# A decode step of attention plus an MLP on one core: K is transposed on VectorE in 32 by 32 blocks instead of on TensorE

## The chip, the cores and the metric

One core of a Trainium2 chip. The metric is the device time of one execution in microseconds. The kernel before takes 134.06 us (median of 8 runs, 133.88 to 134.23).

## What is computed

Two rows (batch 2, one token each, 576 wide) are normalised and go through two branches that are added. Branch A is attention with 32 query heads and 16 key/value heads over the last 2048 positions of a cache; branch B is an MLP of width 4608 with a squared ReLU.

```python
W = min(4096, max(256, Sk // 4))                       # 2048 of Sk = 8192
q = (x @ wq).reshape(B, Sq, Hq, Dh).transpose(0, 2, 1, 3)   # Hq = 32, Dh = 128
k = jnp.repeat(k_cache[:, :, Sk - W:, :], rep, axis=1)      # Hkv = 16, rep = 2
v = jnp.repeat(v_cache[:, :, Sk - W:, :], rep, axis=1)
scores = jnp.einsum("bhqd,bhkd->bhqk", q, k) * (Dh ** -0.5)
o = jnp.einsum("bhqk,bhkd->bhqd", softmax(scores), v)
A = o.transpose(0, 2, 1, 3).reshape(B, Sq, Hq * Dh) @ wo
h = relu(x @ w1 + b1) ** 2
B_ = h @ w2 + b2
out = x0 + A + B_                                      # x = layernorm(x0)
```

All inputs are bf16. 53.6 MB are read: K and V 16.8 MB each, wq and wo 4.7 MB each, w1 and w2 5.3 MB each.

## The kernel before, in words

**Units.** K and V are worked in 8 units u of 4 key/value heads and one batch row. A unit's K, and its V, is one tile of 128 partitions by 8192 elements (2 MB): each partition holds 64 consecutive positions of one head, 128 elements each. Six such tiles share one ring of buffers (`kvpool`, L85); a load into a buffer waits until the tile in it has been read for the last time.

**Loads.** All large loads are issued by SP (SyncE), in program order: k0, wq, k1, v0, k2, v1, k3, v2, k4, v3, k5, v4, k6, v5, w1, k7, v6, v7, wo, w2 in five pieces. wq, w1 and wo share one buffer (`wbig`), so w1 waits until q is computed, and wo until `mlp_h` has read w1.

**One unit.** `transposes` (L258): TensorE turns 128x128 blocks of K seen as 4-byte words (two bf16 each), four to a PSUM tile, 32 in a unit; ScalarE (L270) and VectorE (L272) in turn copy the tiles to SBUF, 8 copies a unit. `scores` (L274) multiplies by q in two halves of the unit, t = 0 and 1, on 32-column strips of TensorE that run side by side: the stationary tile is q for 8 (head, query) columns, placed by zeros (`qz`), and a product with `far_h` first puts a large negative number where head and row do not belong together. `softmax` (L288): VectorE takes the row maximum (m1, L291), spreads it (m2, L293), GpSimd takes the maximum over partitions (L295), VectorE forms the bias (gown, L298), ScalarE the exponential (L302), VectorE transposes the result in 32 by 32 blocks (pT, L305). `pv` (L314) multiplies by V in 16 products; `pv_end` (L326) sums four parts on VectorE (L333, L335); `fin` adds over partitions by a product (op, L341) and divides (L344, L347, L351), which leaves a column block of `ws`.

**Order.** TensorE keeps the program's order (L94, L97). In `step(u)` (L387) the transposes of unit u are interleaved with p·v of unit u-2 and its `fin`; scores(u, 0) comes after the sixth group of transposes, scores(u, 1) and softmax(u) at the end. VectorE's and ScalarE's order is set by a scheduler. After step 6 comes `mlp_h` (L356): 72 products with w1, ReLU on ScalarE (L373), the square on VectorE (hrow, L375), transposes back and copies to `hT_sb` (L384). Then the loads of wo and w2 are issued, and step 7, p·v of units 6 and 7, and the output products follow: 128 with wo (which need all of `ws`), 144 with w2, a cast (L456) and the store.

`q_block` (L226) computes q in 36 products when wq is there, copies it (L238), transposes it (4 products) and writes it into `qz` (L254).

Of the kernel before, what the change touches and what calls it, by code (L numbers as in the profile page):

```python
# [16 lines left out]
def kernel(  # L17
# [32 lines left out]
    JG = 8  # L50
    NG = NJ // JG
# [5 lines left out]
    TG = NG // NT  # L57
    QZ = 2 * NC
    assert SR == 32 and NG % NT == 0

# [34 lines left out]

    def transpose(*a, **k):
        tc.keep_in_program_order(nc.tensor.transpose(*a, **k))  # L97
# [18 lines left out]
    def issue_flat(w, name):  # L116
        n = w.shape[0] * w.shape[1] // P
        tl = wbig.tile([P, NH * L1], BF16, tag="wbig", name=name)
        nc.sync.dma_start(out=tl[:, 0:n], in_=w.rearrange("r n -> (r n)").rearrange("(p l) -> p l", p=P))
        return tl  # L120

    const.tile([P, 144], F32, name="pad_0")
# [15 lines left out]
    tmp_f = work.tile([P, 2, Dh], F32, tag="tmp", name="tmp_f")  # L138
# [50 lines left out]
    nc.vector.tensor_scalar(out=off[:], in0=own[:], scalar1=BIG, scalar2=-BIG, op0=ALU.mult, op1=ALU.add)  # L189
    of_h = const.tile([P, NC * WC], F32, name="of_h")  # L190
# [29 lines left out]

    qz = const.tile([P, NQ, B, 2, 3 * QZ], BF16, name="qz")
    nc.gpsimd.memset(qz[:], 0.0)
# [3 lines left out]
    def q_block():  # L226
        for t in range(NH):
            for g in range(NG4):
                o = t * LQ + g * QW
                matmul(q_ps[32 * g:32 * g + 2 * B, :], lhsT=xnT[:, t].rearrange("p x b -> p (x b)"),  # L230
                       rhs=wq_sb[:, o:o + QW], start=(t == 0), stop=(t == NH - 1), skip_group_check=True,
                       tile_position=(0, 32 * g))
        row_t = const.tile([RB, 4 * HW], BF16, tag="row", name="qrow")
        qrow = row_t[:, 0:2 * QW]
        nh = QH // 2
        for k in range(2):
            cp = nc.scalar.copy if k else nc.vector.tensor_copy
            cp(out=qrow[:, k * QW:(k + 1) * QW].rearrange("p (i a d) -> p i a d", a=2, d=Dh),  # L238
               in_=q_ps[0:RB, k * QW // 2:(k + 1) * QW // 2].rearrange("p (i d) -> p i d", d=Dh).unsqueeze(2)
               .to_broadcast([RB, nh, 2, Dh]))  # L240
        qrow_f = qrow.bitcast(F32)
        qT_ps = psum.tile([P, QH * P], F32, tag="sc", bufs=2, name="qT_ps")
        for i in range(QH):
            transpose(out=qT_ps[:, i * P:i * P + RB], in_=qrow_f[:, i * Dh:(i + 1) * Dh],
                      identity=ident_f[0:RB, 0:RB])
        qT_v = qT_ps[:].bitcast(BF16).rearrange("p (i g e x b c) -> p b x g c e i", g=NG4 // 2, e=2, x=32 // B, b=B, c=2)
        hd = Dh // 2
        for j2 in range(2):
            cp = nc.scalar.copy if j2 else nc.vector.tensor_copy
            pp = slice(hd * j2, hd * (j2 + 1))  # L250
            o = QZ + NC * j2
            for b in range(B):
                for half in range(2):
                    cp(out=qz[pp, half * NQ // 2:(half + 1) * NQ // 2, b, :, o:o + NC].rearrange(  # L254
                        "p g c (e i) -> p g c e i", e=2), in_=qT_v[pp, b, half])

    kT_tiles, sc_tiles, pT_tiles, o1_tiles, o_tiles = {}, {}, {}, {}, {}
    def transposes(u, g):  # L258
        k_f = k_tiles[u][:].bitcast(F32)
        kT_ps = psum.tile([P, JG * P], BF16, tag="kT", bufs=3, name=f"kT_ps_{u}_{g}")  # L260
        kT_f = kT_ps[:].bitcast(F32)
        for i in range(JG // 2):
            j = g * JG // 2 + i
            transpose(out=kT_f[:, i * P:(i + 1) * P], in_=k_f[:, j * P:(j + 1) * P], identity=ident_f[:])
        t, o = divmod(g, TG)
        if o == 0:
            kT_tiles[(u, t)] = ktpool.tile([P, TG * JG * P], BF16, tag="kT_sb", name=f"kT_{u}_{t}")
        kT = kT_tiles[(u, t)][:, o * JG * P:(o + 1) * JG * P]
        if g % 2 == 0:
            nc.scalar.copy(out=kT, in_=kT_ps[:])  # L270
        else:
            nc.vector.tensor_copy(out=kT, in_=kT_ps[:])  # L272

    def scores(u, t):  # L274
        tq, b = divmod(u, B)
        if t == 0:
            sc_tiles[u] = psum.tile([P, NJJ * 32], F32, tag="sc", bufs=2, name=f"sc_ps_{u}")
            matmul(sc_tiles[u][:], lhsT=far_h[:], rhs=is_h, start=True, stop=False, skip_group_check=True)
        sc_ps = sc_tiles[u]
        kT = kT_tiles.pop((u, t))[:].rearrange("p (j k c) -> p j k c", k=P, c=2)  # L280
        z = QZ * (1 - t)
        for c in range(2):
            for g in range(4):
                matmul(sc_ps[32 * g:32 * (g + 1), :], lhsT=qz[:, tq, b, c, z:z + SR],
                       rhs=kT[:, :, 32 * g:32 * (g + 1), c], start=False, stop=(t == NT - 1 and c == 1),
                       skip_group_check=True, tile_position=(0, 32 * g))

    def softmax(u):  # L288
        sc_ps = sc_tiles.pop(u)
        m1 = work.tile([P, 1], F32, tag="m1", name=f"m1_{u}")  # L290
        nc.vector.tensor_reduce(out=m1[:], in_=sc_ps[:], axis=AX.X, op=ALU.max)  # L291
        m2 = work.tile([P, NC], F32, tag="m2", name=f"m2_{u}")
        nc.vector.tensor_scalar(out=m2[:], in0=off[:], scalar1=m1[:, 0:1], scalar2=None, op0=ALU.add)  # L293
        gmax = work.tile([P, NC], F32, tag="gmax", name=f"gmax_{u}")
        nc.gpsimd.partition_all_reduce(gmax[:], m2[:], channels=P, reduce_op=ReduceOp.max)  # L295
        gown = work.tile([P, NC], F32, tag="gown", name=f"gown_{u}")
        bias = work.tile([P, 1], F32, tag="bias", name=f"bias_{u}")
        nc.vector.scalar_tensor_tensor(out=gown[:], in0=gmax[:], scalar=-scale, in1=own[:], op0=ALU.mult,  # L298
                                       op1=ALU.mult, accum_out=bias[:])
        p_sb = work.tile([P, NJJ * 32], BF16, tag="p_sb", bufs=1, name=f"p_{u}")  # L300
        o1 = keep.tile([P, Dh + 1], F32, tag="o1", name=f"o1_{u}")
        nc.scalar.activation(out=p_sb[:], in_=sc_ps[:], func=ACT.Exp, bias=bias[:, 0:1], scale=scale,  # L302
                             accum_out=o1[:, Dh:Dh + 1])
        pT = keep.tile([P, NJJ, SR], BF16, tag="pT", name=f"pT_{u}")
        nc.vector.transpose(out=pT[:].rearrange("p j r -> p (j r)"), in_=p_sb[:])  # L305
        pT_tiles[u] = pT
        o1_tiles[u] = o1
# [6 lines left out]
    def pv(u, part, parts):  # L314
        n = NJJ // parts
        if part == 0:
            o_tiles[u] = psum.tile([P, NS * Dh], F32, tag="o", name=f"o_ps_{u}")
        v = v_tiles[u][:].rearrange("p (t j s d) -> p j t s d", t=NT, s=2, d=Dh)
        for j in range(part * n, (part + 1) * n):
# [3 lines left out]
        if part == parts - 1:  # L323
            pT_tiles.pop(u)

    def pv_end(u):  # L326
# [3 lines left out]
        for k in range(NS):  # L330
            kw = dict(out=o1[:, 0:Dh], in0=o_ps[:, k * Dh:(k + 1) * Dh])
            if k == 0:
                nc.vector.tensor_scalar(scalar1=in_s[:, 0:1], scalar2=None, op0=ALU.mult, **kw)  # L333
            else:
                nc.vector.scalar_tensor_tensor(scalar=in_s[:, k:k + 1], in1=o1[:, 0:Dh], op0=ALU.mult, op1=ALU.add,  # L335
                                               **kw)

        def fin():
# [5 lines left out]
            nc.vector.reciprocal(out=linv[pp, :], in_=op[pp, Dh:Dh + 1])  # L344
            om_t = work.tile([P, Dh], F32, tag="om", name=f"om_{u}")
            om = om_t[pp, :].rearrange("p (q r) -> p q r", r=WR)
            nc.vector.scalar_tensor_tensor(out=om, in0=op[pp, 0:Dh].rearrange("p (q r) -> p q r", r=WR),  # L347
                                           scalar=linv[pp, 0:1], op0=ALU.mult, op1=ALU.mult,
                                           in1=own_c[pp, :].unsqueeze(2).to_broadcast([32, WC, WR]))
            with nc.allow_low_precision(reason="sums of one term and zeros"):  # L350
                nc.vector.tensor_reduce(out=ws[pp, :, BS * b], in_=om.rearrange("p q r -> p r q"), axis=AX.X,  # L351
                                        op=ALU.add)
# [3 lines left out]
    def mlp_h(w1_sb):  # L356
        h_ps = [psum.tile([P, HB], F32, tag="kT", bufs=3, name=f"h_ps_{k}") for k in range(2)]
# [29 lines left out]
    def step(u):  # L387
        fin = None
        w = u - 2
        with_pv = w >= 0  # L390
        for g in range(NG):
            transposes(u, g)
            if with_pv and g == 1:
                pv(w, 0, 2)
            if with_pv and g == 2:
                pv(w, 1, 2)
                fin = pv_end(w)
            if g == TG + 1:
                scores(u, 0)
            if g == TG + 2 and fin:  # L400
                fin()
        scores(u, 1)
        softmax(u)

    def pv_all(u):
        pv(u, 0, 1)
        pv_end(u)()

    for g in range(NG):
        transposes(0, g)  # L410
    q_block()
    for t in range(NT):
        scores(0, t)
    softmax(0)
    load_v(2)
    b1_rows = B_b1.rearrange("(x n) -> x n", n=HW)
# [4 lines left out]
    load_k(4)  # L421
# [16 lines left out]
    nc.sync.dma_start(out=w2a_sb[:], in_=w2_rows[0])  # L438
# [49 lines left out]
```

## Time and profile before

| | |
|---|---|
| median of 8 runs | 134.06 us (133.88 to 134.23) |
| the profiled execution's own time | 134.23 us |
| its span in the profile | 132.3 us |
| TensorE busy (949 products), weight loads | 84.1 us (64%), 52.0 us |
| VectorE busy (176 instructions) | 63.2 us (48%) |
| ScalarE busy (67 instructions) | 46.7 us (35%) |
| GpSimd busy | 4.9 us (4%) |
| HBM read | 53.62 MB, 405 GB/s over the span |
| mean granted TensorE clock | 0.833 |

The span runs from the first instruction to the last; the execution's own time is 1.93 us longer. In the slices each digit is the busy tenth of 1/40 of the span (3.3 us), and the clock row gives the TensorE clock that the throttle granted. The chain of waits is followed back from the last instruction, at each step to what released it. Groups give, after the name and the shape, the count, the busy time in us and the mean in ns, then the idle time ahead of them and what ended it. "PE" is TensorE, "PEld" its weight loads, "DVE" VectorE, "ACT" ScalarE, "POOL" GpSimd, "SPq" SyncE's queue.

### The profile page before, as it was taken

What the parts mean: (1) busy time and instruction counts of PE and PEld (TensorE: products, weight loads), DVE (VectorE), ACT (ScalarE), POOL (GpSimd) and SP (SyncE); (2) the same over time, 40 slices, a digit from 0 to 9 for tenths busy, and PEclk for the clock granted to TensorE, in tenths of its full rate; (3) what the DMA queues carried; (4) which work ended last, traced back from release to release, by engine and by line L of the source; (5) the groups of instructions that cost most, each with busy time, mean ns of one, the idle gap of its engine ahead of it and who ended that gap; (6) DMA issues with size and microseconds to landing.
All of it is one profiled execution on the core that took longest, in us unless ns stands there. A gap on an engine that the chain in (4) does not pass through costs nothing.

```text
span 132.3 us, 2285 instructions
## 1 busy us (share of the span) xinstructions
PE 84.1 (64%) x949; PEld 52.0 (39%) x949; DVE 63.2 (48%) x176; ACT 46.7 (35%) x67; POOL 4.9 (4%) x15
## 2 busy tenths in 40 slices
PE   0079319599589687697599697103829971639461
PEld 0059202276345353363454353002427540229350
DVE  7764400345557677496547587400075667540000
ACT  5715500338566085283256193200106632000000
POOL 5000000010010100100100100100000001000000
PEclk9999955959999999999779999755686999555955
DMA  4999999999999999999999999999999999899960
GB/s 154 381 456 491 402 392 421 436 421 441 418 436 431 436 426 411 446 421 446 421 436 423 431 477 401 481 391 414 431 421 436 485 428 435 382 432 411 413 234 1
DMA packets 3511, 53.76 MB, mean 406 GB/s; under 512 B 419, under 2 KB 558, under 8 KB 814
## 3 DMA queue, kind: packets, MB, share of 16 engines
q1 hardware_dynamic: 3456, 53.61, 95.1%
q8 instruction: 7, 0.11, 0.3%
q10 hardware_dynamic: 46, 0.02, 0.1%
q14 instruction: 2, 0.02, 0.0%
HBM read 53.62 MB, written 0.00 MB: 405 GB/s over the span
## 4 chain that ended last, share of the span: by engine, by line
DMA 78%; PE 15%; SPq 2%; ACT 2%; DVE 1%; issue 1%; ACTq 0%; DVEq 0%
DMA w<-in_B_w_dram 25%; DMA w2c<-in_B_w_dram 24%; DMA k<-in_A_k_cache_dram 16%; DMA wq<-in_A_wq_dram 13%; PE kT_ps L97 5%; PE h_ps L94 3%; PE q_ps L94 3%; PE sc_ps L94 2%; PE out_ps L94 1%; SPq L106 1%; PE o_ps L94 1%; ACT kT L270 1%; DVE qrow L238 1%; ACT qrow L238 0%; DVE qz L254 0%
## 5 line engine op out<-in xcount | busy, mean ns | idle before, releaser
L97 PE MATMUL kT_ps<-ident_f,k 128*128 128x128 f32 x256 | 41.0, 309 | 6.3 <-DMA k<-in_A_k_cache_dram 4.5
L97 PEld LDWEIGHTS kT_ps<-ident_f,k 128*128 128x128 f32 x256 | 32.5, 159 | 19.6 <-issue 10.1
L270 ACT COPY kT<-kT_ps 128x1024 bf16<-128x1024 bf16 x32 | 31.9, 1012 | 17.9 <-PE kT_ps L97 17.9
L272 DVE COPY kT<-kT_ps 128x1024 bf16<-128x1024 bf16 x32 | 21.8, 681 | 6.6 <-PE kT_ps L97 6.4
L94 PE MATMUL sc_ps<-kT,qz 128*32 128x512 bf16 x128 | 10.0, 393 | 6.7 <-DVE kT L272 4.7
L302 ACT ACTIVATE p<-sc_ps,bias 128x512 bf16<-128x512 f32 x8 | 5.5, 688 | 21.3 <-DVE gown L298 21.3
L94 PE MATMUL o_ps<-v,pT 128*32 128x512 bf16 x128 | 11.2, 429 | 0.0
L94 PEld LDWEIGHTS <-xnT 128*4 128x4 bf16 x108 | 3.4, 118 | 16.8 <-issue 15.2
L94 PE MATMUL h_ps<-w,xnT 128*4 128x288 bf16 x72 | 4.1, 413 | 8.2 <-DMA w<-in_B_w_dram 8.2
L305 DVE STREAM_TRANSPOSE pT<-p 128x512 bf16<-128x512 bf16 x8 | 5.7, 710 | 6.2 <-ACT p L302 6.2
L335 DVE SCALAR_TENSOR_TENSOR o<-o_ps,in_s,o 128x128 f32<-128x128 f32 x24 | 8.3, 345 | 0.4
L291 DVE TENSOR_REDUCE m<-sc_ps 128x1 f32<-128x512 f32 x8 | 5.5, 692 | 4.9 <-PE sc_ps L94 4.9
L375 DVE TENSOR_TENSOR hrow<-t 100x1152 bf16<-100x1152 f32 x2 | 2.6, 1356 | 9.6 <-ACT t L373 9.6
L94 PE MATMUL q_ps<-wq,xnT 128*4 128x512 bf16 x36 | 4.0, 627 | 4.6 <-DMA wq<-in_A_wq_dram 4.6
L295 POOL PARTITION_ALL_REDUCE gmax<-m x8 | 2.9, 365 | 105.0 <-DVE m L293 105.0
L456 ACT CAST fin_sb<-out_ps 113x144 bf16<-113x144 f32 x1 | 0.3, 279 | 18.1 <-PE out_ps L94 18.1
L94 PE MATMUL op_ps<-o,of_h 128*32 128x129 f32 x16 | 3.7, 316 | 4.6 <-DVE o L335 4.6
L94 PEld LDWEIGHTS <-qz 128*32 128x32 bf16 x128 | 2.1, 94 | 10.4 <-DVE kT L272 7.2
L97 PE MATMUL pro_ps<-ident,xn_sb 2*128 2x2 bf16 x5 | 0.9, 181 | 6.8 <-DVE xn_sb L171 6.5
L94 PEld LDWEIGHTS <-hT_sb 128*17 128x17 bf16 x144 | 3.3, 107 | 3.9 <-issue 3.9
L94 PE MATMUL out_ps<-wo,ws 128*17 128x144 bf16 x128 | 4.0, 323 | 1.2 <-DVE ws L351 1.2
L238 DVE CAST qrow<-q_ps 100x512 bf16<-100x512 f32 x1 | 0.7, 692 | 7.9 <-PE q_ps L94 7.9
(71 smaller groups left out, 57.5 us busy)
## 6 DMA issues: line engine op xcount, KB each, us to landing
k<-in_A_k_cache_dram SPq DMA_DIRECT2D x8, 2048.0 KB, 21.2
v<-in_A_v_cache_dram SPq DMA_DIRECT2D x8, 2048.0 KB, 21.6
w<-in_B_w_dram SPq DMA_DIRECT2D x1, 5184.0 KB
wq<-in_A_wq_dram SPq DMA_DIRECT2D x1, 4608.0 KB, 17.8
wo<-in_A_wo_dram SPq DMA_DIRECT2D x1, 4608.0 KB
w2a<-in_B_w_dram SPq DMA_DIRECT2D x1, 2592.0 KB, 27.0
w2b<-in_B_w_dram SPq DMA_DIRECT2D x1, 1296.0 KB
w2c<-in_B_w_dram SPq DMA_DIRECT2D x1, 864.0 KB
```

The lines of the kernel that those rows point to most:

```text
L94: tc.keep_in_program_order(nc.tensor.matmul(*a, **k))
L97: tc.keep_in_program_order(nc.tensor.transpose(*a, **k))
L106: nc.sync.dma_start(out=tl[:], in_=cache[b, tq * TH:(tq + 1) * TH, S0:Sk, :].rearrange("h (c j) d -> c h (j d)", c=CP))
L238: cp(out=qrow[:, k * QW:(k + 1) * QW].rearrange("p (i a d) -> p i a d", a=2, d=Dh), in_=q_ps[0:RB, k * QW // 2:(k + 1) * QW // 2].rearrang ...
L270: nc.scalar.copy(out=kT, in_=kT_ps[:])
L272: nc.vector.tensor_copy(out=kT, in_=kT_ps[:])
L291: nc.vector.tensor_reduce(out=m1[:], in_=sc_ps[:], axis=AX.X, op=ALU.max)
L295: nc.gpsimd.partition_all_reduce(gmax[:], m2[:], channels=P, reduce_op=ReduceOp.max)
L302: nc.scalar.activation(out=p_sb[:], in_=sc_ps[:], func=ACT.Exp, bias=bias[:, 0:1], scale=scale, accum_out=o1[:, Dh:Dh + 1])
L305: nc.vector.transpose(out=pT[:].rearrange("p j r -> p (j r)"), in_=p_sb[:])
L335: nc.vector.scalar_tensor_tensor(scalar=in_s[:, k:k + 1], in1=o1[:, 0:Dh], op0=ALU.mult, op1=ALU.add, **kw)
L375: nc.vector.tensor_tensor(out=h4[:, :, k * HB:(k + 1) * HB], in0=t4, in1=t4, op=ALU.mult)
```

## The change

K is transposed on VectorE. One instruction turns half a unit, 2048 4-byte words on each of 128 partitions, in blocks of 32 by 32, from SBUF to SBUF; there are two in a unit. A head vector is 64 words; a block puts 32 of them on the 32 partitions of one quarter, and the rows that lay in that quarter stay in it. So the scores need a stationary tile that is block-diagonal over the four quarters: 128 columns, in which each quarter's 32 rows hold the same half of q for the 8 (head, query) columns of that quarter, and zeros elsewhere. `q_place` (one VectorE product with a 0/1 pattern `own_p`) writes that tile for each unit into one of two buffers. A unit's scores are now 16 products of 128 columns over 512, one for each fourth of a partition's positions, half of the vector and element of the pair, instead of 16 on 32-column strips. The 256 TensorE transposes of K and their 64 copies are gone. q is copied four times side by side and transposed in eight products; V's positions follow the new order in `pv`.

VectorE's instructions of the loop now keep the program's order too. `softmax` is cut in two: row maximum, spread and partition maximum come first, then `fin` of unit u-2, q_place(u+1) and the first half of K of unit u+1, then the rest of the softmax (bias, exponential, pT), then the second half of K of unit u+1. p·v of unit u-2 comes ahead of the scores of u, in one part. k4 is issued ahead of step 1, and the issues of w1, wo and w2's first half keep their place. In VectorE's compiled order the two hrow squares of `mlp_h` stand after q_place(7) and ahead of the first half of K of unit 7. `mlp_h`'s PSUM tiles have two buffers of their own.

```diff
+    dve = tc.keep_in_program_order
...
-    qz = const.tile([P, NQ, B, 2, 3 * QZ], BF16, name="qz")
-    nc.gpsimd.memset(qz[:], 0.0)
+    qc = const.tile([P, NQ, B, NA, NC], BF16, name="qc")
+    qz = [const.tile([P, NA, P + QO], BF16, name=f"qz_{k}") for k in range(2)]
+    for k in range(2):
+        nc.gpsimd.memset(qz[k][:], 0.0)
...
+    def q_place(u):
+        tq, b = divmod(u, B)
+        sh = [P, NA, NP4, NC]
+        dve(nc.vector.tensor_tensor(out=qz[u % 2][:, :, QO:].rearrange("p a (q c) -> p a q c", c=32)[:, :, :, 0:NC],
+                                    in0=qc[:, tq, b].unsqueeze(2).to_broadcast(sh),
+                                    in1=own_p[:].unsqueeze(1).unsqueeze(3).to_broadcast(sh), op=ALU.mult))
...
-        for i in range(JG // 2):
-            j = g * JG // 2 + i
-            transpose(out=kT_f[:, i * P:(i + 1) * P], in_=k_f[:, j * P:(j + 1) * P], identity=ident_f[:])
...
-        if g % 2 == 0:
-            nc.scalar.copy(out=kT, in_=kT_ps[:])
-        else:
-            nc.vector.tensor_copy(out=kT, in_=kT_ps[:])
+    def transposes(u, t):
+        kT = ktpool.tile([P, UE // NT], BF16, tag="kT_sb", name=f"kT_{u}_{t}")
+        n = UE // NT // 2
+        tc.keep_in_program_order(nc.vector.transpose(out=kT[:].bitcast(F32),
+                                                     in_=k_tiles[u][:].bitcast(F32)[:, t * n:(t + 1) * n]))
+        kT_tiles[(u, t)] = kT
...
-        for c in range(2):
-            for g in range(4):
-                matmul(sc_ps[32 * g:32 * (g + 1), :], lhsT=qz[:, tq, b, c, z:z + SR],
-                       rhs=kT[:, :, 32 * g:32 * (g + 1), c], start=False, stop=(t == NT - 1 and c == 1),
-                       skip_group_check=True, tile_position=(0, 32 * g))
+        for i in range(NS // NT):
+            z = QO - NC * (t * NS // NT + i)
+            for h in range(2):
+                for e in range(2):
+                    matmul(sc_ps[:], lhsT=qz[u % 2][:, 2 * h + e, z:z + P], rhs=kT[:, i, :, h, :, e], start=False,
+                           stop=(t == NT - 1 and i == NS // NT - 1 and h == 1 and e == 1), skip_group_check=True)
...
     def step(u):
-        fin = None
         w = u - 2
-        with_pv = w >= 0
-        for g in range(NG):
-            transposes(u, g)
-            if with_pv and g == 1:
-                pv(w, 0, 2)
-            if with_pv and g == 2:
-                pv(w, 1, 2)
-                fin = pv_end(w)
-            if g == TG + 1:
-                scores(u, 0)
-            if g == TG + 2 and fin:
-                fin()
-        scores(u, 1)
-        softmax(u)
+        if w >= 0:
+            pv(w)
+        for t in range(NT):
+            scores(u, t)
+        fin = pv_end(w) if w >= 0 else None
+        rest = softmax(u)
+        if fin:
+            fin()
+        if u + 1 < NU:
+            q_place(u + 1)
+            transposes(u + 1, 0)
+        rest()
+        if u + 1 < NU:
+            transposes(u + 1, 1)
...
-    for g in range(NG):
-        transposes(0, g)
+    for t in range(NT):
+        transposes(0, t)
     q_block()
-    for t in range(NT):
-        scores(0, t)
-    softmax(0)
+    q_place(0)
+    step(0)
     load_v(2)
+    load_k(4)
```

## The prediction

> **What bounds the kernel now.** I read the slices first, then the chain of waits, then the groups by shape, then the time rows of the tail, and last the granted clock in stretches that I chose.
>
> ```profile
>
> DMA  4999999999999999999999999999999999899960
> GB/s 154 381 456 491 402 392 421 436 421 441 418 436 431 436 426 411 446 421 446 421 436 423 431 477 401 481 391 414 431 421 436 485 428 435 382 432 411 413 234 1
> ```
>
> The DMA engines are full from the second slice to the last but two. 53.6 MB in the 126 us from 2.0 to 128 is 425 GB/s: a K or V load (2.10 MB) takes 4.93 us of the stream, wq and wo 11.1, w1 and w2 12.5 each.
>
> ```profile
> 58.18 33.19 DMA w<-in_B_w_dram
> ...
> 91.41 4.11 PE h_ps L94 x66
> ...
> 95.53 0.33 SPq L119
> ...
> 96.86 31.21 DMA w2c<-in_B_w_dram
> ...
> 128.12 1.45 PE out_ps L94 x31
> 129.57 0.02 issue
> 129.59 0.28 ACT fin_sb L456
> ```
>
> These are the chain's rows (start, length). Compute matters at two places. The issue of wo at 95.53 waits for mlp_h, since w1 and wo share one buffer. wo and w2 are 10.0 MB, 23.6 us of stream that ends at 128.07, so the queue still held work until 104.5: wo could come some 7.7 us later, with 1.3 us from issue to flow (k0: issued at 0.73, flowing at 2.0). The second place is the tail:
>
> ```profile
> 118.42 3.98 PE L94 MATMUL out_ps<-wo,ws 128*17 128x144 bf16 x128 [1.16 <-DVE ws L351]
> 122.98 1.05 PE L94 MATMUL out_ps<-w2a,hT_sb 128*17 128x144 bf16 x54 [0.58 <-DMA w2a<-in_B_w_dram]
> 126.06 1.26 PE L94 MATMUL out_ps<-w2b,hT_sb 128*17 128x144 bf16 x36 [0.48 <-DMA w2b<-in_B_w_dram]
> 128.12 1.43 PE L94 MATMUL out_ps<-w2c,hT_sb 128*17 128x144 bf16 x36 [0.80 <-DMA w2c<-in_B_w_dram]
> ```
>
> The wo product starts when the last softmax, p·v and merge are done (118.4), not when wo lands; after that TensorE waits for w2. Without those waits its 272 products would take about 6.8 us (31 ns each in the half-clock row of 128, 19 ns in the full-clock row of 54, about half and half) and end at 125.2: 4.3 us of slack. So the compute chain may slip by about 4 us for nothing, and then each microsecond counts in full.
>
> **What is removed.**
>
> ```profile
> L97 PE MATMUL kT_ps<-ident_f,k 128*128 128x128 f32 x256 | 41.0, 309 | 6.3 <-DMA k<-in_A_k_cache_dram 4.5
> L270 ACT COPY kT<-kT_ps 128x1024 bf16<-128x1024 bf16 x32 | 31.9, 1012 | 17.9 <-PE kT_ps L97 17.9
> L272 DVE COPY kT<-kT_ps 128x1024 bf16<-128x1024 bf16 x32 | 21.8, 681 | 6.6 <-PE kT_ps L97 6.4
> L305 DVE STREAM_TRANSPOSE pT<-p 128x512 bf16<-128x512 bf16 x8 | 5.7, 710 | 6.2 <-ACT p L302 6.2
> L144 DVE STREAM_TRANSPOSE row<-tmp_f 128x32 f32<-128x32 f32 x1 | 0.2, 163 | 0.0
> ```
>
> TensorE, ScalarE and VectorE lose 41.0, 31.9 and 21.8 us busy (the first three rows). All of it lies beside a full DMA queue, so by itself it is worth nothing. The cover is the stream, 9.87 us per K and V pair: the kernel before needs 8.95 us a unit (its row maxima m start at 73.94 and 82.89).
>
> **What is added: 16 transposes of 128x2048 4-byte words.** The two last rows bound the price. 512 elements in 710 ns are 533 ns at 0.96 per ns plus 177 fixed, so 2048 take 2.31 us. A line through both rows (1.14 ns an element) gives 2.46. [...] I take 2.31. VectorE's work on K grows from 2.7 to 4.6 us a unit, and lies in one strict line with the softmax.
>
> **The new cycle**, from the end of unit u's scores to the end of the next, in VectorE's new order (durations from the rows of 72 to 86 us): m1 0.74 with its wait, m2 0.27, the three of fin 1.04, q_place 0.34, first half transposed 2.35, gown 0.29, the wait for the exponential 0.93, pT 0.71, second half 2.35. Together 9.0. Then eight products that need the second half. Before, four column strips ran side by side: 8 products of 32 columns in 0.62 us. Now each is 128 wide and they go one by one: 512 columns at the rate that 0.62 implies [...] are 8 x 0.216 + 0.19 + 0.1 = 2.0. Sum 11.0 us at full clock, 10.0 where there is no fin (two steps). pv_end (1.5 us) lies beside the eight products. q_place is shown nowhere: at most 0.35 (the 128-element rows at L335), at least 0.15 (L189); I take 0.30. That spread over 6 steps is about 1 us.
>
> 11.0 is more than the stream's 9.87, so VectorE and TensorE in turn become the slower side.
>
> **Start.** q is computed at 23.3 as before. Then qrow is twice as long and goes VectorE then ScalarE (1.23 and 1.01 us, against 0.69 and 0.59), eight transposes instead of four, q_place: q is in place at 27.3 instead of 26.0. Sixteen scores products take 3.5 us at full clock, 6.8 at half; the clock was half from 26.8 to 30 and I expect it there again: scores of unit 0 end at 32.3 (27.3 before). Unit 0's transposes (8.4 to 13.2) are under the wq load.
>
> **The clock.** [...] Full-clock stretches with the stretches that follow:
>
> ```profile
> 50.60:54.00 3.40, 2.14 (x22) 1.04 (x18) 2.21 (x7) 1.01 (x1) 0.00 (x0) 1.00 0.99 424
> ...
> 60.80:64.30 3.50, 1.21 (x13) 0.47 (x12) 2.53 (x6) 0.71 (x1) 0.33 (x1) 0.99 1.03 440
> 64.30:67.70 3.40, 3.21 (x18) 2.08 (x19) 1.58 (x4) 1.79 (x3) 0.03 (x1) 0.51 1.01 434
> ...
> 122.20:125.60 3.40, 1.73 (x80) 1.18 (x73) 0.00 (x0) 0.00 (x0) 0.00 (x0) 1.00 1.00 419
> 125.60:129.00 3.40, 2.15 (x68) 1.87 (x68) 0.00 (x0) 0.00 (x0) 0.00 (x0) 0.51 0.62 241
> ```
>
> Columns: length, TensorE busy, weight loads, VectorE, ScalarE, GpSimd, clock, DMA. After 1.21 or 1.73 us of work in a stretch the next one is at half clock (0.51); after 2.14 it stays full. Now a cycle of 11 us has 5.6 us of TensorE work (twice 1.9, p·v 1.05, mask and op 0.4 each) in two bursts, with holes of 3.0 and 2.4 us that the transposes before filled: about half, at the edge. By the row alone, always full, a step is 11.0; [...]always half, 8 products take 3.4 instead of 1.7 and a step is 12.7. A half-clock stretch is busier and lifts the clock again, so it should alternate. I take a third: 0.6 us a step.
>
> **Sum.** Scores of unit 6 end at 32.3 + 2 x 10.0 + 4 x 11.0 = 96.3 at full clock, and 6 x 0.6 later, 99.9, as I expect. mlp_h follows (0.5 for op and its first load, then 2.2 at full clock or 4.1 as measured at half; I take 3.1): it ends at H = 103.5, against 95.5. w1 lands at 91.4 and no longer matters. After H, VectorE: relu and the two hrow 3.0, first half of unit 7 2.35, gown and a copy to hT 0.6, pT after the exponential 1.35, second half 2.35, three copies 1.3, pv_end 1.5, m1 and m2 1.0, fin 1.0, gown to pT 1.9, pv_end of unit 6 1.6, op and p·v of unit 7 1.6, its pv_end, op and fin 3.3: 22.9, as long as the stretch before (95.5 to 118.4), since K's last transposes stand in for the copies. Then the 272 products, 6.8 us now without DMA waits, end at H + 29.7; cast and store need 2.75 (129.55 to 132.3). Span H + 32.5 = 136.0. The profiled run took 134.23 for a span of 132.3 (the median of the runs is 134.06), so the time is 137.9; I say 138.0. Break-even is at H = 99.8.
>
> **The queue.** SP's waits for K buffers now end with a second-half transpose: k4 at 40.4, k5 at 51, k6 at 62, at most 3 later with the slow clock; the loads issued ahead of each land at 48.8, 58.6 and 68.5. V buffers come free at 45, 55, 66, with 7 us in hand. Behind each stand only later loads. So the stream does not dry up there. wo is issued at H; if later than 103.2 the stream pauses, but it then ends at H + 24.9, ahead of TensorE's H + 29.7. load_k(4) ahead of step 1, the fixed order of the wo and w2a issues, own_p (0.3 us in VectorE's 0.84 us hole at 5.1), two memsets on GpSimd (1.2 us, needed at 27) and the tile sizes cost nothing: all are covered by the loads of k0 and wq.
>
> **Rivals.**
> - The chain fits (0.25): score products and mlp_h nearly all at full clock, H = 99.0. For it: 4 us of slack; a busy tail at full clock would take 36 products in 0.7 instead of 1.43, as TensorE no longer waits cold. Time 133.5. Against it: the two half-full windows above. It decides if the mean step from unit 2 on is at most 11.0 us. This is the faster side, and part of it comes out within 0.2%.
> - Much slower (0.09): half clock throughout gives H = 113, a tail of 34 and 152 us[...].
> - My forecast has 0.66, with its own range 135 to 143.
>
> A measurement tells 0.2% (0.27 us) from no change. Faster 0.18 and same 0.07 are the first rival; slower 0.75 is the rest. The range 133.4 to 144 takes in the first rival, the line-through price (14 x 0.15 = 2.1) and a clock loss of up to 1.2 a step.
>
> **What would show it.** Right: transposes near 2.3 us; row maxima 11 to 12 us apart from unit 2; h_ps ending near 103; wo's product starting near 126 with w2c already landed; DMA idle in the last 6 us; a chain that ends over VectorE and TensorE instead of DMA. Wrong: the chain still ending in w2c at 128; steps under 10.5; clock 1.0 in every slice from 30 to 100; or transposes over 2.6 us.

## The result and the profile after

The changed kernel takes 1.0088 of the time before (95% interval 1.0068 to 1.0109): about 135.2 us against 134.03. Its eleven executions lie between 134.87 and 139.5 us (median 138.78), those of the kernel before between 133.88 and 134.77, and the ratio compares only the executions within 1.5% of the quickest of their kernel. So two executions of the changed kernel are read here: the one on record (138.15 us, span 136.1) and a later one of the unaltered kernel (135.28 us, span 133.2).

The slices of the 135.28 us execution, and its chain by engine:

```profile
DMA  4999999999999999999999999989999999999920
GB/s 143 394 448 488 399 395 443 423 433 433 428 431 423 433 423 438 423 438 428 433 433 433 433 468 491 423 360 403 448 413 443 485 432 421 399 436 402 409 98 6
...
## 4 chain that ended last, share of the span: by engine, by line
DVE 43%; PE 30%; DMA 13%; ACT 6%; issue 4%; SPq 0%; ACTq 0%
```

The chain of the kernel before, by engine:

```profile
DMA 78%; PE 15%; SPq 2%; ACT 2%; DVE 1%; issue 1%; ACTq 0%; DVEq 0%
```

The load stream is as full as before (DMA row) and ends at about the same time (its last packets are in at 128.7 us, 128.9 before), now 4.5 us ahead of the end of the span instead of 3.5. The chain that ends last no longer runs over the loads (DMA 13% instead of 78%) but over VectorE and TensorE in turn. The groups that replace TensorE's transposes, from the page of the 138.15 us execution:

```profile
L94 PE MATMUL sc_ps<-kT,qz 128*128 128x512 bf16 x128 | 43.7, 504 | 22.1 <-DVE gown L300 15.4
L271 DVE STREAM_TRANSPOSE kT<-k 128x2048 f32<-128x2048 f32 x16 | 36.5, 2283 | 0.0
```

The score products were a quarter as wide before:

```profile
L94 PE MATMUL sc_ps<-kT,qz 128*32 128x512 bf16 x128 | 10.0, 393 | 6.7 <-DVE kT L272 4.7
```

ScalarE falls from 46.7 to 15.8 us busy, VectorE rises from 63.2 to 81.2. The tail of the 135.28 us execution by time (start, length), to be held against the four rows of before:

```profile
105.42 5.75 PE L94 MATMUL sc_ps<-kT,qz 128*128 128x512 bf16 x16
...
122.46 4.02 PE L94 MATMUL out_ps<-wo,ws 128*17 128x144 bf16 x128 [1.16 <-DVE ws L352]
126.25 1.26 PE L94 MATMUL out_ps<-w2a,hT_sb 128*17 128x144 bf16 x50
128.73 0.55 PE L94 MATMUL out_ps<-w2a,hT_sb 128*17 128x144 bf16 x22 [1.21 <-issue]
129.05 0.79 PE L94 MATMUL out_ps<-w2b,hT_sb 128*17 128x144 bf16 x36
129.61 0.79 PE L94 MATMUL out_ps<-w2c,hT_sb 128*17 128x144 bf16 x36
```

No product waits for w2 any more. The wo product starts at 122.46 (118.42 before), and TensorE ends at 130.4 instead of 129.6. In the 138.15 us execution it starts at 126.86. Yet h_ps ends at 95.1 in the quicker execution, earlier than before (95.5), and at 99.6 in the other. So 27.4 and 27.3 us lie between the end of h_ps and the wo product, where before it was 22.9.

After this my theory was that the compute chain sets the end, by two separate faults. The step's length depends on where the half-clock stretches fall, which differs from execution to execution; and all 16 score products of unit 7 run late, in one piece. The rivals are VectorE's transposes alone, with no part for the clock, and the load stream.

### The profile page after: what moved, and what is told of

It reads as the page before. It is cut to its first block, busy times and chain, and to the rows that moved or that the text cites. A ratio compares the mean times of both kernels' runs of the same rounds, so it can differ in the third digit from the quotient of the medians.

```text
span 136.1 us, 1729 instructions
## 1 busy us (share of the span) xinstructions
PE 77.8 (57%) x697; PEld 33.1 (24%) x697; DVE 81.2 (60%) x169; ACT 15.8 (12%) x35; POOL 5.3 (4%) x16
## 4 chain that ended last, share of the span: by engine, by line
DVE 42%; PE 33%; DMA 13%; ACT 6%; issue 3%; SPq 0%; ACTq 0%
DVE kT L271 23%; PE sc_ps L94 20%; DMA wq<-in_A_wq_dram 13%; PE out_ps L94 5%; DVE pT L307 4%; ACT p L304 4%; DVE m L291 4%; PE q_ps L94 3%; DVE hrow L376 2%; PE h_ps L94 2%; DVE ws L352 2%; DVE o L336 2%; DVE om L348 2%; PE o_ps L94 1%; DVE qz L263 1%
## 5 line engine op out<-in xcount | busy, mean ns | idle before, releaser
L94 PE MATMUL sc_ps<-kT,qz 128*128 128x512 bf16 x128 | 43.7, 504 | 22.1 <-DVE gown L300 15.4
L271 DVE STREAM_TRANSPOSE kT<-k 128x2048 f32<-128x2048 f32 x16 | 36.5, 2283 | 0.0
L94 PEld LDWEIGHTS <-qz 128*128 128x128 bf16 x128 | 15.0, 119 | 49.7 <-issue 39.2
L94 PE MATMUL o_ps<-v,pT 128*32 128x512 bf16 x128 | 12.9, 481 | 0.0
L245 DVE CAST qrow<-q_ps 100x1024 bf16<-100x1024 f32 x1 | 1.2, 1224 | 10.0 <-PE q_ps L94 10.0
L94 PEld LDWEIGHTS <-pT 128*32 128x32 bf16 x128 | 4.5, 112 | 3.2 <-issue 1.6
L99 PE MATMUL hp<-ident,hrow 100*128 100x100 bf16 x18 | 1.7, 256 | 5.4 <-DVE hrow L376 3.1
L94 PEld LDWEIGHTS <-ws 128*17 128x17 bf16 x128 | 3.7, 135 | 1.6 <-issue 1.6
L94 PE MATMUL sc_ps<-ident,far_h 4*128 4x512 bf16 x8 | 3.5, 436 | 0.9 <-ACT hT_sb L385 0.9
L94 PEld LDWEIGHTS op_ps<-o,of_h 128*32 128x32 f32 x16 | 1.3, 124 | 10.7 <-issue 10.3
```

The costliest lines, as they stand in the source:

```text
L94: tc.keep_in_program_order(nc.tensor.matmul(*a, **k))
L245: cp(out=qrow[:, h * 2 * QW:(h + 1) * 2 * QW].rearrange("p (i a d) -> p i a d", a=NP4, d=HD), in_=q_v[:, h].unsqueeze(2).to_broadcast([RB, ...
L271: tc.keep_in_program_order(nc.vector.transpose(out=kT[:].bitcast(F32), in_=k_tiles[u][:].bitcast(F32)[:, t * n:(t + 1) * n]))
```

## The experiments

**The changed kernel once more.**

> The changed kernel once more, unaltered, for more executions with their granted clock. Theory (the compute chain sets the end, and the place of the half-clock windows on it differs from execution to execution): times spread again from about 135 to 139.5, and the longer an execution, the lower its mean clock (0.79 at 139, 0.85 or more at 135). Rival (the chain of VectorE's transposes alone sets the end, the clock plays no part): times and clocks are unrelated. Rival (the load stream sets the end): times within 0.3 us of each other.

Measured: 134.26 to 139.47 us, median 138.03, ratio 1.0042 (1.0016 to 1.0067). With the first set, all six executions under 135.7 us have a mean clock of 0.846 to 0.872, all twelve over 137 us one of 0.788 to 0.824. The load stream alone does not give such a spread: the kernel before, with the same loads, has 36 executions between 133.88 and 134.39 us on the same chip. That the clock causes it is shown by the filling products below. Where the half clock falls is seen in the score products of one step, first in the 138.15 us execution, then in the 135.28 us one (first half, second half of the unit; eight products each):

```profile
56.87 3.57 PE L94 MATMUL sc_ps<-kT,qz 128*128 128x512 bf16 x8 [2.77 <-DVE gown L300]
60.76 2.90 PE L94 MATMUL sc_ps<-kT,qz 128*128 128x512 bf16 x8 [0.32 <-DVE kT L271]
```

```profile
55.55 3.36 PE L94 MATMUL sc_ps<-kT,qz 128*128 128x512 bf16 x8 [2.77 <-DVE gown L300]
59.44 1.90 PE L94 MATMUL sc_ps<-kT,qz 128*128 128x512 bf16 x8 [0.53 <-DVE kT L271]
```

At full clock eight take 1.90, at half clock 3.57 (the first row; the clock is 0.50 from 56.0 to 62.8 us there). The first half may take 3.4 for nothing, since VectorE is on the second half of K meanwhile. The second half is on the path: 2.90 instead of 1.90 is 1.0 us lost. In the quick execution the step (10.1 to 10.3 us) is close to three stretches of 3.4 us, the least time between two changes of the clock in the traces of the kernel before and of the 138.15 us execution (before: 1.00 from 94.92 to 98.33 us, 0.50 to 101.74, 1.00 to 111.98), and the half clock falls on the first half of each of units 3 to 6.

**hp in other PSUM buffers.**

```diff
-            hp = psum.tile([P, nr, RB + 4], BF16, tag="sc", bufs=2, name=f"hp_{a}")
+            hp = psum.tile([P, nr, RB + 4], BF16, tag="h", bufs=2, name=f"hp_{a}")
```

> One word is changed: the two PSUM tiles of the MLP's transposes (hp) take the buffers of h_ps instead of those of the scores, so unit 7's scores no longer wait for the copies of hp. Theory: in the profile of the changed kernel all 17 score products of unit 7 ran after the last hp copy had begun (109.4 to 115.6); freed, the first half runs under the second transpose and the row maximum comes 2 (full clock) to 4 us (half clock) earlier, the tail from the end of h_ps to the wo product falls from 27.3 to 23 to 25 us, and the time to 133.8 to 136. Rival (transposes and clock alone): no change beyond 0.5 us.

Measured: 133.9 to 136.02 us in 22 executions, median 134.2, ratio 1.0019 (1.0002 to 1.0037). The three over 135.7 us have a clock of 0.796, so the fault of the clock is still there. The score tile of unit 7 used the two buffers that hp also used. In the changed kernel (135.28 us) TensorE waits for the last copy of the first hp tile:

```profile
101.98 2.19 DVE kT L271
104.20 0.32 DVE hT_sb L385
104.55 0.32 ACT hT_sb L385
104.86 0.04 issue
104.91 6.28 PE sc_ps L94 x17
111.21 0.70 DVE m L291
```

These are rows of its chain: K's second half is ready at 104.2, the scores end at 111.2. With the edit, by time:

```profile
101.21 0.60 PE L94 MATMUL sc_ps<-ident,far_h 4*128 4x512 bf16 x1
...
101.74 4.37 PE L94 MATMUL sc_ps<-kT,qz 128*128 128x512 bf16 x16
101.89 2.27 DVE L271 STREAM_TRANSPOSE kT<-k 128x2048 f32<-128x2048 f32 x1
...
106.15 0.69 DVE L291 TENSOR_REDUCE m<-sc_ps 128x1 f32<-128x512 f32 x1
```

The first eight run under the transpose, the row maximum comes at 106.15 instead of 111.2, h_ps to wo product is 22.3 us, and the chain ends in w2's landing at 128.03 again. The 135.28 us execution and this one are alike up to there (row maximum of unit 6 at 92.12 and 92.11), so the 5 us come from this wait. About 2 of them are half clock on products that the wait has put on the path: the 16 took 5.75 us together, where twice eight at full clock take 3.8 (the clock is 0.50 from 100 to 105 us and 0.66 on average from 105 to 112).

**Filling products, and both edits.** The filling products, in units 1 to 6 (with both edits, to 7):

```diff
+    def fill(n):
+        for i in range(n):
+            matmul(fill_ps[:], lhsT=fill_w[:], rhs=qc[:].rearrange("p a b c d -> p (a b c d)").unsqueeze(1)
+                   .to_broadcast([P, 2, NQ * B * NA * NC]), start=True, stop=True, skip_group_check=True)
...
+            if 0 < u < NU - 1:
+                fill(8)
+        elif 0 < u < NU - 1:
+            fill(5)
```

> Added work whose result nobody reads: in units 1 to 6 eight products of 128 by 512 on a zero tile ahead of each unit's first eight score products and five ahead of the second eight, into an own PSUM bank, to fill TensorE's holes and keep its clock up. Theory (clock): steps at full clock, 11.0 us each, unit 6's scores end near 96 in every execution, the spread shrinks to the tail's share, mean clock above 0.88; time 135 to 137. Rival (the clock plays no part): the products only add TensorE work; time as before or up to 2 us longer. If the fill products themselves stand in the way, steps become longer than 11.3 us at clock 1.0.

> Both edits together, and the filling products in unit 7 too. Theory: the chain then ends ahead of the load stream or with it; h_ps ends near 99, the wo product starts near 122 to 123, TensorE waits for w2 or just catches up, and the time is 133.4 to 134.2 with a small spread, about as the kernel before or a little under. Rival (VectorE's transposes alone): 135 or more, since none of VectorE's work is taken away.

Measured: the fill alone 134.8 to 135.21 us in five executions, ratio 1.0066 (1.0054 to 1.0078), clock 0.91 to 0.92; both edits 133.93 to 134.34 in 13, ratio 1.0004 (0.9996 to 1.0012). With the fill, every half of scores in units 1 to 6 takes 1.89 to 1.91 us. The 11.0 us a step that I still expected was wrong: the row maxima are 9.2 apart in the first two steps, then 10.1 to 10.3. The rows of one step with the fill (the first has the last four of its eight filling products):

```profile
53.76 1.03 PE L94 MATMUL fill_ps<-qc,fill_w 128*128 128x512 bf16 x4
55.73 1.90 PE L94 MATMUL sc_ps<-kT,qz 128*128 128x512 bf16 x8 [0.95 <-DVE gown L313]
57.47 1.24 PE L94 MATMUL fill_ps<-qc,fill_w 128*128 128x512 bf16 x5
59.62 1.89 PE L94 MATMUL sc_ps<-kT,qz 128*128 128x512 bf16 x8 [0.91 <-DVE kT L271]
```

Work that nobody needs makes the kernel faster at the median (135.07 against 138.03 on the same chip), so the clock is the cause of the spread, not only a companion. The two edits take away the two faults separately: the fill the spread, hp's buffers the rest.

In unit 7 the filling products are not free. With both edits eight of them run from 101.2 to 103.5 us, unit 7's first scores only then, and its row maximum comes 16.6 us after that of unit 6 (91.51 and 108.06), against 14.0 with hp's buffers alone (92.11 and 106.15). The load stream hides this here: the time is level with the kernel before.

**The second half of w2 not loaded.** Its products read the first half, so the second half of w2 is left out of the result; TensorE's work is the same, the stream 6.2 us shorter (2.65 MB at the 425 GB/s of the kernel before). The same edit in the kernel before, the changed one, and the one with both edits:

```diff
-    nc.sync.dma_start(out=w2b_sb[:], in_=w2_rows[1, :, 0:R9 * D])
-    for r0, r1 in W2P:
-        nc.sync.dma_start(out=w2c_sb[:, (r0 - R9) * D:(r1 - R9) * D], in_=w2_rows[1, :, r0 * D:r1 * D])
...
-        w, o = (w2b_sb, r) if r < R9 else (w2c_sb, r - R9)
+        w, o = w2a_sb, r
```

> The kernel before with the second half of w2 not loaded (2.65 MB, 6.2 us of the stream at 425 GB/s); its products read the first half instead, so TensorE's work is unchanged and the second half of w2 is left out of the result. Theory (the load stream sets this kernel's end, and its compute chain ends 4.3 us earlier): the wo product starts at 118.4 as before, TensorE ends near 125.2 instead of 129.6, time 129.5 to 130.5. Rival (the stream and the chain end together already): less than 1 us gained.

> The changed kernel with the same load left out. Theory (its compute chain sets the end): it gains little; in an execution whose steps lose nothing to the clock the wo product starts near 122.5 and TensorE ends near 129 (132.9 to 133.7 in time); in the others the time is as with all loads, up to 139. Rival (the stream sets the end): 4 us gained, as in the kernel before.

> The changed kernel with both edits (hp in the buffers of h_ps, filling products in units 1 to 7) and the same load left out. Theory: the wo product starts near 119.3 and TensorE ends near 125, time 129 to 130.5, level with the kernel before under the same cut: the mended change gives the compute chain no lead over the kernel before, even where the stream is out of the way. Rival (TensorE's and ScalarE's freed time is worth something once the stream is shorter): below 129.

Measured, each against the kernel before with all loads: before 130.31 us, ratio 0.9721 (0.9697 to 0.9744); changed 134.37 in one execution and 139.4 to 139.5 in three; both edits 131.31, ratio 0.9794 (0.9752 to 0.9836). The kernel before is bound by its loads and gains 3.7 us. The changed one gains nothing against its own executions of the same mean clock with all loads (0.858: 134.37 against 134.26 and 134.52; 0.789: 139.4 to 139.5 against 139.2 to 139.5), so its end is not the stream's. With both edits the gain is 2.8, and the kernel stays about 1 us behind: its wo product starts at 120.05, that of the kernel before at 118.93.

That this shows no lead of the change would be too much said, for the filling products of unit 7 are in it: K's second half is ready at 104.2 us, but the eight scores that need it start behind five of them.

```profile
101.79 2.40 PE L94 MATMUL fill_ps<-qc,fill_w 128*128 128x512 bf16 x8
104.03 1.90 PE L94 MATMUL sc_ps<-kT,qz 128*128 128x512 bf16 x8
105.77 1.24 PE L94 MATMUL fill_ps<-qc,fill_w 128*128 128x512 bf16 x5
106.85 1.91 PE L94 MATMUL sc_ps<-kT,qz 128*128 128x512 bf16 x8
```

In the one trace with hp's buffers alone and all loads, the row maximum of unit 6 comes at the same time (92.11, here 92.16), and the wo product starts at 117.40. That is 1.0 us ahead of the kernel before with all loads (118.42) and 1.5 ahead of it with the shorter stream. That version was not run with the shorter stream, so whether the change is then ahead stays open.

**Filling the tail too.** With both edits, filling products during the merges of units 6 and 7, ahead of the wo product and in the waits for w2; then without those in the waits; then four in one wait only, without any others.

```diff
         pv(u)
+        fill(5)
         pv_end(u)()
...
+    fill(4)
     for r in range(WR):
         out_acc(ws[:, r, :], wo_sb, r)
     for r in range(FR):
         out_acc(hT_sb[:, 0, r, :], w2a_sb, r)
+    fill(6)
     for r in range(FR):
         w, o = (w2b_sb, r) if r < R9 else (w2c_sb, r - R9)
+        if r == R9:
+            fill(4)
```

> Both edits, and filling products in the tail too: five each while p.v of units 6 and 7 is merged, four ahead of the wo product, six and four in the waits for the second half of w2. Theory (the last products run at half clock, 36 in 1.3 us, only because TensorE waits cold for the last load): at full clock they take 0.7, the end comes 0.5 us earlier, time near 133.6, under both kernels. Rival (the fill delays the wo product or the last products): 134.1 or more.

> As the kernel with filling products in the tail, without the ten in the waits for w2; those during the merges of units 6 and 7 and ahead of the wo product stay. Theory (what cost time there was work queued in the waits for w2, behind which the last products start late): level with the kernel before, 133.9 to 134.3, in every execution. Rival (the fill in the merges, or more instructions on TensorE as such, which stops for 1 to 2 us with no wait shown): spread up to 136 or more again.

> The changed kernel with hp in the buffers of h_ps and only four filling products, in the wait for the second half of w2. Theory (TensorE's last 36 products run cold): if they warm the clock, 0.3 to 0.5 us are gained in the undisturbed executions, 133.6; four are 1.7 us at half clock and fit a wait of 1.5 to 1.9 us. Rival (too little to move the clock): as without them, 133.9 to 136.

Measured: 134.06 to 137.69 us, ratio 1.0043 (1.0024 to 1.0061); 133.93 to 134.99, ratio 1.0019 (1.0008 to 1.003); 134.06 to 137.15, ratio 1.0054 (1.0027 to 1.0081). The half microsecond was not to be had, and none of the three kept to the times of its theory. In the first, the ten executions from 136.5 us up have a clock of 0.937 to 0.961, so the half clock is not what makes them long; none of them has a trace. The first of the three, by time (135.07 us):

```profile
124.08 0.39 PE L94 MATMUL fill_ps<-qc,fill_w 128*128 128x512 bf16 x1
126.59 1.25 PE L94 MATMUL fill_ps<-qc,fill_w 128*128 128x512 bf16 x5 [2.12 <-issue]
127.77 0.74 PE L94 MATMUL out_ps<-w2b,hT_sb 128*17 128x144 bf16 x36
128.44 1.04 PE L94 MATMUL fill_ps<-qc,fill_w 128*128 128x512 bf16 x4
129.41 0.74 PE L94 MATMUL out_ps<-w2c,hT_sb 128*17 128x144 bf16 x36
```

The last products do run at full clock (36 in 0.74 us, against 1.26 and 1.43 in the kernel before), but TensorE stops for 2.12 us in which it waits for nothing that the profile shows, and the filling products then stand ahead of the work. Such a stop of 0.4 to 1.2 us is in six other tails too, that of the kernel before among them.

Counted along TensorE's program, the stop stands in all seven behind product 603, 731 or 859. These are 128 apart: the filling products push the place along, and it falls on the same count again. In the kernel before, a 16 KB packet of a queue that the profile calls "instruction" (q8) starts at 122.66 us, 2.43 us before the stop ends at 125.09. In the 138.15 us execution one starts at 128.36 us; TensorE comes to the place behind product 603 only 3.3 us later, at 131.63, and there is no stop. What TensorE waits for in the stop, and whether the packet has a part in it, is not shown; no run was made to test it. No version here beats the kernel before.

## Why the prediction was wrong

The direction was right, the size was not: 138.0 was forecast, 3.9 us more than before, and the ratio stands for 135.2, 1.2 more. The step that failed is the sum up to H, the end of mlp_h: it had the step of a unit too long and put a loss to the clock on the path, and H came at 95.1 instead of 103.5. The tail behind it was too short by 5.6. That the median of all executions, 138.8, lies near 138.0 is chance: in the 138.15 us execution H comes 3.9 us early, and the stretch from there to the wo product is 4.4 too long.

**What held.** The load stream bounds the kernel before, and its compute chain has 4 us to spare (3.7 gained without half of w2). The 94.7 us of engine work that were removed brought no time in any version here. A transpose takes 2.28 us (2.31 forecast: 710 ns for 512 elements and 1536 more at 0.96 per ns, the rate between the two rows below). The bound moves to VectorE and TensorE in turn, wo's issue never starves the stream, and the K and V loads are issued in time: k4 at 40.6, k5 at 50.7, k6 at 60.7 in the 138.15 us execution (40.4, 51 and 62 forecast). The two rows, from the page of the kernel before, are VectorE's for 512 elements (692 ns) and for 1152 (1356 ns), 640 elements in 664 ns:

```profile
L291 DVE TENSOR_REDUCE m<-sc_ps 128x1 f32<-128x512 f32 x8 | 5.5, 692 | 4.9 <-PE sc_ps L94 4.9
L375 DVE TENSOR_TENSOR hrow<-t 100x1152 bf16<-100x1152 f32 x2 | 2.6, 1356 | 9.6 <-ACT t L373 9.6
```

**The step, "Sum 11.0 us at full clock", was 10.1 to 10.3.** I added whole durations and a gap for each instruction. On VectorE the next one begins before the recorded end of the one ahead (q_place, the row qz, runs from 83.73 to 84.02 us, the transpose behind it starts at 83.94), and each counts for less in the chain of a step (135.28 us execution):

```profile
83.73 0.29 DVE qz L263
84.02 2.22 DVE kT L271
86.24 0.07 DVE gown L300 x2
86.31 0.02 issue
86.33 0.04 ACTq L304
86.37 0.05 issue
86.42 0.79 ACT p L304 x2
87.21 0.02 issue
87.23 0.71 DVE pT L307
87.94 2.20 DVE kT L271
90.15 0.04 issue
90.19 1.90 PE sc_ps L94 x8
```

A transpose counts 2.2 and not 2.35, gown 0.07 and not 0.29, the eight products 1.94 and not 2.0 (with the fill, four products of 512 columns take 1.03 us and five 1.24, so 0.21 each, against 0.216 forecast). The six steps are 59.2 us (row maxima 32.88 to 92.12), where 64 were forecast: 4.8 too many. From unit 2 on a step is 10.2 us on average, and "steps under 10.5" was one of the prediction's own signs of being wrong.

**The clock, "I take a third: 0.6 us a step".** In the 135.28 us execution it costs nothing on the path of the six steps, 3.6 us less than forecast. The half clock came: the stretch from 51.7 to 55.1 us has 1.06 us of TensorE work, and the clock is 0.55 from 54.8 to 58.2 us, with 2.65 us of work, and 0.95 from 58.2 to 61.6. So the half clock followed a stretch with little work, as in the forecast's rows of the kernel before. How little makes the difference is not shown: behind 1.5 us of work in a stretch the clock was half in the 138.15 us execution (1.49 from 52.6 to 56.0 us, then 0.50 to 62.8) and full in this one (38.1 to 41.5; the 16 p·v products at 42.12 take 1.05 us, those at 102.12, at a clock of 0.50, 1.90). That a busier half-clock stretch lifts the clock again was my estimate from one row: in the kernel before the clock was 1.00 behind 3.21 us of work (64.3 to 67.7 us), but stayed at 0.50 behind 2.32 (112.0 to 115.4). But which eight products it hits decides: the first half is hidden, the second is not. An average hid that this is one of two cases. In the 138.15 us execution the six steps are 63.3 us, 4.1 more. mlp_h, at full clock (1.00 from 92.0 to 95.5 us in the 135.28 us execution), ends 3.0 us after unit 6's scores instead of 3.6.

H is thus 95.1 and not 103.5 (4.8, 3.6 and 0.6 less, and the first unit's scores 0.6 later than forecast), which is before the break-even at 99.8, and the first rival, "the chain fits", would have come about but for the tail (134.2 with hp in other buffers, if not the 133.5 it named).

**The tail after H, "22.9, as long as the stretch before", was 27.4.** I took it that unit 7's first score products run under the second transpose. Their PSUM tile was waiting for the copies of hp, since both take turns in two buffers, and I had not asked which tiles share those. The kernel before has the same sharing, but there the first scores of unit 7 come at 105.0, after the last hp copy (102.65), and eight products take 0.62 us. So the wo product starts 4.0 us later than before, within the 4.3 of slack.

**"The 272 products, 6.8 us now" took 7.9.** The rest is the stop of 1.2 us, with which TensorE ends 0.8 us later than before (130.4 against 129.6). The tail of the kernel before has such a stop, in a row that the prediction does not list:

```profile
125.09 0.48 PE L94 MATMUL out_ps<-w2a,hT_sb 128*17 128x144 bf16 x18 [1.06 <-issue]
```

There it lay inside the wait for w2 and cost nothing, and I put it at nothing for the new tail as well. By this reckoning the longer tail alone nearly used up the slack in the quick execution, and the stop took the rest and 0.8 us more.

## What to carry to other kernels

Work removed from engines beside a full load stream was worth nothing here, but the work put in its place can use up the slack of the chain behind; measure that slack in two places, at the issue that frees a shared buffer and at the last product, before the engine totals, and count the stops for which the profile shows no wait. When products get longer (eight took 0.62 us, now 1.90), look at every tile that takes turns with their output tile. Where TensorE has little work in a 3.4 us stretch (here the half clock came behind 0.56 to 1.73 us of it), ask which products the half clock will hit rather than how many.

## What the runs showed of the hardware that was not expected

The same program spread over 3.9% (134.26 to 139.5 us) on one core by the place of its half-clock stretches (mean clock 0.846 to 0.872 under 135.7 us, 0.788 to 0.824 over 137), and 78 idle-filling products brought that to 0.3% (134.8 to 135.21). TensorE stopped for 0.4 to 2.1 us among the output products with no wait shown, in seven traces always behind product 603, 731 or 859 of its program, 128 apart.
